# Moving a search's VectorE operands to PSUM and its work into earlier waits, in a balanced expert layer

## The chip, the cores and the metric

The kernel runs on one core of a Trainium2 chip. The metric is the time of one execution on the device in microseconds (us). Runs of one kernel here differ by up to some 1.5%, so all comparisons are between a kernel's fast runs and the runs of the kernel before in the same rounds on the same chip.

## The reference

Linear attention with a root-mean-square norm feeds a layer of eight experts, in which every expert takes exactly 576 of the 4608 tokens. The assignment is greedy over the logits in falling order:

```python
kv = np.einsum('bhsd,bhse->bhde', k, v)                  # batch 8, heads 8, seq 576, dim 64
out = np.einsum('bhsd,bhde->bhse', q, kv)
attn = out / sqrt(mean(out * out) + 1e-06) * g_norm      # -> x: 4608 x 512
...
order = np.argsort(-(x @ w_gate).flatten())              # 4608 * 8 logits
for idx in order:
    tok, e = int(idx) // E, int(idx) % E
    if assigned[tok] >= 0 or counts[e] >= cap:           # cap = 576
        continue
    assigned[tok] = e; counts[e] += 1
for e in range(E):
    out[assigned == e] = np.maximum(x[assigned == e] @ w1[e], 0.0) @ w2[e]
```

## The kernel before: the parts that matter

The kernel doesn't sort. It fills one expert at a time. For each it finds a threshold of the logits by a search of seven steps; in a step TensorE counts, for 32 candidate thresholds at once, how many tokens lie over each, and VectorE picks the interval and compares again. The chosen tokens become a list, GpSimd gathers their rows from DRAM (`xg`), VectorE scales them (`xs`), TensorE transposes them for the expert's matmuls (`xt`; this is the "turn").

All of it for the later experts is woven into TensorE's program between the matmuls of the earlier expert's two layers. A generator yields a distance, in us of TensorE's matmuls, after which its next piece is put into the program; the programs of TensorE, VectorE and ScalarE then have a fixed order.

```python
def threshold(t, over):                      # the search of expert t
    ...
    for s in range(NSTEP):
        yield 4.6 if s > 0 else 0.4 if first else 2.0 if t == 1 else 4.0
        n_ps = bank([P, E, G], "n_ps")
        for c in range(0, GC, G):            # "the counting": nine small matmuls
            nc.tensor.matmul(n_ps, lhsT=over[:, c:c + G]..., rhs=best[:, :, c:c + G], ...)
        ...                                  # VectorE: need, full, some, some_t, kk, ends: the interval
        compare(over, candidates(s + 1, lo, cand_ps))     # "over", 1.35 us, what the next counting reads
...
def fetch(t, which, index):                  # the list
    ...
    yield 3.2 if t == 1 else 4.2 if t < E - 1 else 2.4
    ...                                      # a_ps: matmuls, then know and since on VectorE
    yield 1.6
    ...                                      # s_ps: matmuls, then less, ids, got on VectorE
    for n, (_, nr) in enumerate(blocks):     # five blocks of up to 128 rows
        xg = moe.tile([P, H, W], FT, name="xg", tag="xg", bufs=NB)
        tokens = nc.gpsimd.indirect_dma_start(out=xg[0:nr]..., in_=x_dram, in_offset=...ids...)
    yield "tokens"
    yield 1.5
    ...                                      # up, at_row, half, outs: the rows of the output
def control(t):
    ...                                      # threshold, assign, fetch, later
    for _ in choice():                       # best expert of each token left, for the next search
        yield 0.9
    compare(compared[t + 1], candidates(0, ...))
...
def turn(t):
    def scale(n):
        xs = moe.tile([P, H * D], FT, name="xs", tag="xs")          # two buffers
        nc.vector.tensor_tensor(xs..., xg[0:nr, :, 0:D], xg[0:nr, :, D:D + 1].to_broadcast(...), op=AL.mult)
    scale(0); scale(1)
    yield
    for n, (a, nr) in enumerate(blocks):
        ...                                  # four transposes, ScalarE copies to xt
        if n + 2 < NB:
            scale(n + 2)
        yield
...
hold = 5.0                                   # the turn's first two scalings are put in 5 us after the list
```

## Time and profile before

The kernel took 711.39 us (median of three runs, 709.41 to 716.79). The trace falls into the part up to the first expert's matmuls and eight stretches, one for each expert; stretches 0 to 6 carry the searches and turns. In the lines of profiles below, PE is TensorE (PEld its loading of weights), DVE VectorE, ACT ScalarE and POOL GpSimd. A line of a timeline gives the start and length in us, the engine, the line of the kernel, the operation, output<-inputs, sizes and count, and in brackets the engine's idle time before it and what ended that.

| part of the span before (709.6 us) | us | TensorE busy, us | TensorE idle, us |
|---|---|---|---|
| up to the first matmul of expert 0 | 180.3 | | |
| stretches 0 to 6 | 459.9 | 450.6 | 9.4 |
| rest (stretch 7 and the end) | 69.3 | | |

### The profile page before, as it was taken

Reading aid. Unit: us, or ns where it says so; the run is one execution under the profiler, and the core shown is the slowest. Engines: PE = TensorE matmul, PEld = TensorE weight load, DVE = VectorE, ACT = ScalarE, POOL = GpSimd, SP = SyncE. Lnnn points to the kernel's source line nnn. Section 1 sums busy time; section 2 is a strip of 40 time slices with the busy share of each in tenths; the row PEclk is TensorE's granted clock in tenths of the full one; section 3 lists DMA queues with packets and bytes.
Section 4 is the critical chain, followed back from the end, with each engine's and each line's share of the span. In section 5 each row is a group of like instructions: output and inputs, shape, how many; then the busy total and the mean of one; then the engine's idle time right before and its main releaser. Section 6 shows DMA issues by size and latency. Waiting matters only on the chain.

```text
span 709.6 us, 13280 instructions
## 1 busy us (share of the span) xinstructions
PE 616.8 (87%) x5370; PEld 482.7 (68%) x5370; DVE 443.3 (62%) x1393; ACT 155.9 (22%) x315; POOL 263.8 (37%) x249
## 2 busy tenths in 40 slices
PE   3787788214999899989998999999899999999994
PEld 2566666212778677857885788678677867877782
DVE  4344656888687778888878779887887545020011
ACT  1454555300211121022102111121112022112100
POOL 0100011002342562438344632735263659226322
PEclk9988977555999999999999999999999999999998
DMA  8987889405303600531081053108013843001001
GB/s 283 316 278 237 278 297 351 177 0 184 129 1 103 251 26 1 205 137 38 6 306 67 1 180 132 68 1 312 28 41 127 293 165 106 0 30 38 0 1 67
DMA packets 41405, 93.41 MB, mean 132 GB/s; under 512 B 3456, under 2 KB 3456, under 8 KB 41344
## 3 DMA queue, kind: packets, MB, share of 16 engines
q1 hardware_dynamic: 34752, 72.49, 29.1%
q0 software_dynamic: 5888, 20.06, 8.1%
q8 instruction: 42, 0.69, 0.4%
q14 instruction: 19, 0.16, 0.1%
q10 hardware_dynamic: 704, 0.02, 0.1%
HBM read 72.50 MB, written 20.05 MB: 130 GB/s over the span
## 4 chain that ended last, share of the span: by engine, by line
PE 74%; DVE 13%; issue 6%; DMA 4%; ACT 1%; POOL 1%; POOLq 0%; ACTq 0%; DVEq 0%
PE h_ps L798 35%; PE y_ps L847 20%; PE o_ps L370 3%; PE qt_ps L301 3%; PE y_ps L858 3%; PE kv_ps L313 3%; PE t_ps L747 2%; DVE over L266 2%; DMA xg<-x_dram,ids 2%; PE n_ps L478 2%; DVE xs L733 1%; DMA gw<-in_moe_w_gate_dram 1%; PE warm_ps L625 1%; DVE need L484 1%; DVE held_ps L524 1%
## 5 line engine op out<-in xcount | busy, mean ns | idle before, releaser
L798 PE MATMUL h_ps<-xt,w_sb 128*128 128x288 f32 x1024 | 260.1, 410 | 0.8 <-ACT xt L750 0.8
L798 PEld LDWEIGHTS h_ps<-xt,w_sb 128*128 128x128 f32 x1024 | 190.6, 190 | 55.4 <-issue 5.7
L801 ACT ACTIVATE hid<-h_ps 128x288 f32<-128x288 f32 x128 | 52.6, 411 | 208.1 <-PE h_ps L798 208.1
L847 PE MATMUL y_ps<-tw,sh 128*128 128x256 f32 x384 | 86.5, 380 | 0.0
L847 PEld LDWEIGHTS y_ps<-tw,sh 128*128 128x128 f32 x384 | 72.0, 190 | 9.3
L789 POOL TENSOR_TENSOR sh<-hid 128x512 f32<-128x512 f32 x32 | 41.7, 1303 | 94.4 <-ACT hid L801 94.3
L673 POOL DMA_INDIRECT xg<-x_dram,ids x40 | 38.6, 964 | 82.8 <-DVE ids L668 35.8
L750 ACT ACTIVATE xt<-t_ps,g_col 128x512 f32<-128x512 f32 (+1 forms) x40 | 25.8, 645 | 161.6 <-PE t_ps L747 161.6
L847 PE MATMUL y_ps<-w_sb,hid 128*128 128x256 f32 x256 | 57.8, 381 | 0.0
L266 DVE TENSOR_TENSOR over<-mx,held_ps 128x1152 bf16<-128x1152 f32 x42 | 56.9, 1354 | 1.5
L818 DVE TENSOR_TENSOR y_sb<-y_ps,u 128x512 f32<-128x512 f32 x24 | 16.4, 684 | 63.8 <-PE y_ps L847 63.8
L756 POOL DMA_INDIRECT out_dram<-y_sb,outs x32 | 33.4, 1043 | 52.1 <-issue 36.7
L847 PEld LDWEIGHTS y_ps<-w_sb,hid 128*128 128x128 f32 x256 | 48.1, 190 | 6.6
L524 DVE TENSOR_SCALAR held_ps<-held_ps,width 32x2 f32<-32x2 f32 x144 | 41.3, 287 | 5.3
L779 POOL TENSOR_TENSOR tw<-w_sb 128x512 f32<-128x512 f32 x32 | 39.9, 1269 | 12.4 <-DMA w_sb<-in_moe_w_dram 12.3
L478 PEld LDWEIGHTS <-over 128*128 128x128 bf16 x441 | 17.5, 97 | 38.8 <-DVE over L266 27.5
L370 PE MATMUL o_ps<-kvx,qt 64*64 64x72 f32 x1152 | 32.9, 261 | 9.8 <-issue 9.2
L733 DVE TENSOR_TENSOR xs<-xg 128x512 f32<-128x512 f32 (+1 forms) x40 | 31.9, 809 | 14.7 <-DMA xg<-x_dram,ids 8.1
L478 PE MATMUL n_ps<-best,over 128*128 128x32 bf16 x441 | 19.3, 179 | 21.1 <-DVE over L266 19.2
L370 PEld LDWEIGHTS o_ps<-kvx,qt 64*64 64x64 f32 x1152 | 26.8, 160 | 15.5 <-issue 14.1
L378 DVE TENSOR_REDUCE ms<-sq 128x8 f32<-128x512 f32 x36 | 24.1, 681 | 20.1 <-ACT sq L376 19.9
L327 POOL COPY kvx<-kv 64x512 f32<-64x512 f32 x16 | 9.8, 609 | 71.3 <-DVE kv L321 70.9
(203 smaller groups left out, 831.9 us busy)
## 6 DMA issues: line engine op xcount, KB each, us to landing
w_sb<-in_moe_w_dram SPq DMA_DIRECT2D x16, 1024.0 KB, 6.3
w_sb<-in_moe_w_dram SPq DMA_DIRECT2D x8, 2048.0 KB, 13.3
k_sb<-in_k_dram SPq DMA_DIRECT2D x16, 576.0 KB, 5.4
v_sb<-in_v_dram SPq DMA_DIRECT2D x16, 576.0 KB, 5.8
q_sb<-in_q_dram SPq DMA_DIRECT2D x16, 576.0 KB, 5.6
x_dram<-o_sb SPq DMA_DIRECT2D x16, 576.0 KB, 4.3
x_dram<-o_sb SPq DMA_DIRECT2D x4, 288.0 KB, 4.2
xg<-x_dram,ids POOLq DMA_INDIRECT x40, 5.4
```

What stands on the lines that cost most here:

```text
L266: nc.vector.tensor_tensor(over[:, c0:c1], mx[:, c0:c1].rearrange("p (c o) -> p c o", o=1).to_broadcast([P, c1 - c0, NCAND]), cand[:, 1:NCA ...
L370: nc.tensor.matmul(o_ps[n * HP:(n + 1) * HP, rp, (2 * r2 + l) * W:(2 * r2 + l + 1) * W], lhsT=turned_q[bn][ks, block // 2, l * HP:(l + 1) ...
L478: nc.tensor.matmul(n_ps, lhsT=over[:, c:c + G].rearrange("p c n -> p (c n)"), rhs=best[:, :, c:c + G], start=(c == 0), stop=(c == GC - G))
L524: nc.vector.tensor_scalar(ends[g * QP:(g + 1) * QP], in0=kk, scalar1=width[0:QP, s:s + 1], scalar2=lo_was[0:QP], op0=AL.mult, op1=AL.add)
L673: tokens = nc.gpsimd.indirect_dma_start(out=xg[0:nr].rearrange("p h w -> p (h w)"), out_offset=None, in_=x_dram, in_offset=bass.IndirectOf ...
L733: nc.vector.tensor_tensor(xs[0:nr].rearrange("p (h d) -> p h d", h=H), xg[0:nr, :, 0:D], xg[0:nr, :, D:D + 1].to_broadcast([nr, H, D]), op ...
L756: put = nc.gpsimd.indirect_dma_start(out=out, out_offset=bass.IndirectOffsetOnAxis(ap=ids_of[t][0:nr, n:n + 1], axis=0), in_=y_sb[0:nr, :] ...
L779: in_order(nc.gpsimd.tensor_tensor(o[:, m:m + 2], x[:, m:m + 2], y[:, m:m + 2], op=AL.subtract))
L789: in_order(nc.gpsimd.tensor_tensor(o[:, ms], x[:, ms], y[:, ms], op=op))
L798: nc.tensor.matmul(h_ps, lhsT=w1[:, 2 * (d % 2) + d // 2, f * P:(f + 1) * P], rhs=xt[:, d, cs], start=(d == 0), stop=(d == DC - 1))
L801: nc.scalar.activation(hid[:, f, cs], h_ps, ACT.Relu)
L847: nc.tensor.matmul(p_ps[:, n], lhsT=left[:, f, n * P:(n + 1) * P], rhs=right[:, f], start=(f == 0), stop=(f == FH - 1))
```

## The change

Its intent is twofold. First, GpSimd is busy beside VectorE, and VectorE operations with two operands in SBUF took longer there (`xs` 865 ns in the mean from 181 to 640 us, 690 from 160 to 181 us, where GpSimd did no tensor operation); so each such operation of the search gets an operand in PSUM. Second, the choice for the next search (`choice`) is done inside the waits for the list, in place of behind it, and the computation of the output's rows is cut into six pieces (`deferred`) that go one by one into the next search's steps. The distances are shortened to match.

```diff
-    def bank(shape, nm):
-        return psm.tile(shape, FT, name=nm, tag="c", bufs=1)
+    given = psm.tile([P, 512], FT, name="given_ps", tag="c", bufs=1)
     held = psm.tile([P, 512], FT, name="held_ps", tag="s", bufs=1)
...
+    for nm, shape in (("n", (E, G)), ("all", (3, E)), ("a", (GC + 1,)), ("rise", (2, GC)), ("inv", (2, H)), ("s", ...)):
+        small_ps[nm] = given[:, at:at + n]
...
-            yield 4.6 if s > 0 else 0.4 if first else 2.0 if t == 1 else 4.0
-            n_ps = bank([P, E, G], "n_ps")
+            yield 4.6 if s > 0 else 0.4 if t < 2 else 2.4
+            n_ps = small_ps["n"]
...
+                if deferred:
+                    deferred.pop(0)()
...
-        yield 5.4
+        yield 5.0 if t == 1 else 5.4
...
-    def fetch(t, which, index):
+    def fetch(t, which, index, later):
+        ch = choice() if 0 < t < E - 1 else iter(())
...
-        yield 3.2 if t == 1 else 4.2 if t < E - 1 else 2.4
+        if t > 0:
+            later()
+        yield 2.8 if t < E - 1 else 2.4
...
-        yield 1.6
+        next(ch, None)
+        yield 1.3
...
-            yield 1.5
+            yield 0.7
...
+        deferred.extend([lambda: ...code_left, lambda: climb(0), lambda: climb(1), ...at, half_rows, rows])
+        for _ in ch:
+            yield 0.5
...
+            inv = xg[:, :, D:D + 1]
+            if t > 0:
+                inv = small_ps["inv"][:, n % 2].rearrange("p (h o) -> p h o", o=1)
+                nc.vector.tensor_copy(inv[0:nr], xg[0:nr, :, D:D + 1])
             nc.vector.tensor_tensor(xs[0:nr]..., xg[0:nr, :, 0:D],
-                                    xg[0:nr, :, D:D + 1].to_broadcast([nr, H, D]), op=AL.mult)
+                                    inv[0:nr].to_broadcast([nr, H, D]), op=AL.mult)
```

`held` is a bank that only VectorE uses.

More of the change, by code (lines that the diff above doesn't have):

```diff
@@ L449 @@
                       ("own", (GC,)), ("shut", (E,)), ("code", (E,)), ("some", (2 * QP,)), ("some_t", (2, QP + 1)),
-                      ("kk", (2,)), ("which", (1,)), ("over_room", (E,)), ("last", (E,)), ("is_full", (E,))):
+                      ("kk", (2,)), ("which", (1,)), ("over_room", (E,)), ("last", (E,)), ("is_full", (E,)), ("half", (NB,))):
         n = shape[0] * (shape[1] if len(shape) > 1 else 1)
@@ L455 @@
         at += n
+    at = 0
+    for nm, shape in (("n", (E, G)), ("all", (3, E)), ("a", (GC + 1,)), ("rise", (2, GC)), ("inv", (2, H)), ("s", (NB, GC + 3))):
+        n = shape[0] * (shape[1] if len(shape) > 1 else 1)
+        small_ps[nm] = given[:, at:at + n]
+        if nm == "s":
+            small_ps["mid"] = given[:, at:at + E * GC].rearrange("p (e c) -> p e c", e=E)
+        if len(shape) > 1:
+            small_ps[nm] = small_ps[nm].rearrange("p (t n) -> p t n", t=shape[0])
+        at += n
+    nc.vector.tensor_copy(small_ps["rise"], rise)
     nc.vector.memset(small_ps["some_t"][0:QP, 0, QP:QP + 1], 1.0)
@@ L464, in pieces @@
         return sm[:, 0:2], sm[:, 2:]
+    deferred = []
     def threshold(t, over):
@@ L545, in assign @@
             nc.vector.scalar_tensor_tensor(cut[:, 1], in0=mx, scalar=ends[1], in1=cut[:, 1], op0=AL.is_ge, op1=AL.mult)
-        two = asg.tile([P, 2, E, GC], BF, name="two", tag="two")
-        for n in range(2):
-            nc.vector.tensor_tensor(two[:, n], best, bc_c(cut[:, n]), op=AL.mult)
+        upper, mid = asg.tile([P, E, GC], BF, name="upper", tag="upper"), small_ps["mid"]
         sums = small("sums", 2 * E, BF)
-        with nc.allow_low_precision("counts of up to GC are exact in bf16"):
-            nc.vector.reduce_sum(out=sums, in_=two.rearrange("p t e c -> p (t e) c"), axis=AXX)
-        yield 5.4
-        all_ps = bank([P, 3, E], "all_ps")
+        for n, part in enumerate((upper, mid)):
+            nc.vector.tensor_tensor(part, best, bc_c(cut[:, n]), op=AL.mult)
+            with nc.allow_low_precision("counts of up to GC are exact in bf16"):
+                nc.vector.reduce_sum(out=sums[:, n * E:(n + 1) * E], in_=part, axis=AXX)
+        for do in deferred:
+            do()
+        deferred.clear()
+        yield 5.0 if t == 1 else 5.4
+        all_ps = small_ps["all"]
         nc.tensor.matmul(all_ps[:, 0], lhsT=ones_b, rhs=sums[:, 0:E], start=True, stop=True)
@@ L558, in assign @@
         nc.tensor.matmul(all_ps[:, 2], lhsT=before, rhs=sums[:, E:2 * E], start=True, stop=True)
-        mid = two[:, 1]
         here = asg.tile([P, E, GC], FT, name="here", tag="here")
@@ L589, in later @@
                 nc.vector.tensor_copy(small_ps["code"], code)
-            nc.vector.scalar_tensor_tensor(gone, in0=took, scalar=NONE, in1=gone, op0=AL.mult, op1=AL.add)
+            nc.vector.tensor_scalar(small_ps["mine"], in0=took, scalar1=NONE, scalar2=None, op0=AL.mult)
+            nc.vector.tensor_tensor(gone, gone, small_ps["mine"], op=AL.add)
             nc.vector.tensor_scalar(room, in0=over_room, scalar1=0.0, scalar2=None, op0=AL.max)
@@ L640, in fetch @@
         nc.vector.tensor_tensor_scan(along, ones_b[:, 0:GC], own, 0.0, op0=AL.mult, op1=AL.add)
-        yield 3.2 if t == 1 else 4.2 if t < E - 1 else 2.4
-        a_ps = bank([P, GC + 1], "a_ps")
+        if t > 0:
+            later()
+        yield 2.8 if t < E - 1 else 2.4
+        a_ps = small_ps["a"]
         nc.tensor.matmul(a_ps[:, 0:1], lhsT=before, rhs=along[:, GC - 1:GC], start=True, stop=True)
@@ L652, in fetch @@
             nc.vector.tensor_tensor(since, slot_f, a_ps[:, 0:1].to_broadcast([P, NB * P]), op=AL.is_ge)
-        yield 1.6
-        s_ps = bank([P, NB, GC + 3], "s_ps")
+        next(ch, None)
+        yield 1.3
+        s_ps = small_ps["s"]
         for n in range(NB):
@@ L683, in fetch, with climb, half_rows, rows @@
             yield "tokens"
-            yield 1.5
+            yield 0.7
         up = asg.tile([P, NB, 2, GC], FT, name="up", tag="up")
-        for n in range(2):
-            nc.vector.tensor_tensor(up[:, :, n], less, rise[:, n].rearrange("p (o c) -> p o c", o=1).to_broadcast([P, NB, GC]),
-                                    op=AL.mult)
         at = asg.tile([P, NB, 2], FT, name="at_row", tag="at_row")
-        nc.vector.reduce_sum(out=at, in_=up, axis=AXX)
-        half = small("half", NB)
-        nc.vector.tensor_scalar(half, in0=at[:, :, 1], scalar1=S - 1.0, scalar2=-(S - 1.0), op0=AL.mult, op1=AL.add)
-        nc.vector.tensor_tensor(half, half, got[:, :, 1], op=AL.mult)
-        nc.vector.tensor_tensor(half, half, at[:, :, 0], op=AL.add)
+        half = small_ps["half"]
         outs = asg.tile([P, NB], I32, name="outs", tag="outs", bufs=3)
-        nc.vector.scalar_tensor_tensor(outs, in0=got[:, :, 0], scalar=float(R), in1=half, op0=AL.mult, op1=AL.add)
         ids_of[t] = outs
-        nc.vector.scalar_tensor_tensor(code_left, in0=code, scalar=which, in1=code_left, op0=AL.not_equal, op1=AL.mult)
+        def climb(n):
+            nc.vector.tensor_tensor(up[:, :, n], less, (rise if t == 0 else small_ps["rise"])[:, n].rearrange(
+                "p (o c) -> p o c", o=1).to_broadcast([P, NB, GC]), op=AL.mult)
+        def half_rows():
+            nc.vector.tensor_scalar(half, in0=at[:, :, 1], scalar1=S - 1.0, scalar2=-(S - 1.0), op0=AL.mult, op1=AL.add)
+            nc.vector.tensor_tensor(half, half, got[:, :, 1], op=AL.mult)
+        def rows():
+            nc.vector.tensor_tensor(half, half, at[:, :, 0], op=AL.add)
+            nc.vector.scalar_tensor_tensor(outs, in0=got[:, :, 0], scalar=float(R), in1=half, op0=AL.mult, op1=AL.add)
+        deferred.extend([
+            lambda: nc.vector.scalar_tensor_tensor(code_left, in0=code if t == 0 else small_ps["code"], scalar=which,
+                                                   in1=code_left, op0=AL.not_equal, op1=AL.mult),
+            lambda: climb(0), lambda: climb(1), lambda: nc.vector.reduce_sum(out=at, in_=up, axis=AXX), half_rows, rows])
+        if t == 0:
+            later()
+        if not 0 < t < E - 2:
+            for do in deferred:
+                do()
+            deferred.clear()
+        for _ in ch:
+            yield 0.5
     compared = {0: over0}
@@ L710, in control @@
             yield "weights"
-        yield from fetch(t, which, index)
-        later()
-        pause = None if t == 0 else 0.9
-        if t + 1 < E:
+        yield from fetch(t, which, index, later)
+        if t == 0:
             for _ in choice():
-                yield pause
-            yield pause
+                yield None
+        yield None if t == 0 else 0.5
         if t + 1 < E - 1:
```

## The prediction

> **What bounds the kernel now**
>
> I read the page first (engine shares and the chain that ended last), then the busy time by stretch, with one stretch for each expert's two matmul layers, then the timeline of TensorE for its pauses, and last the timelines of VectorE, GpSimd and the DMA around those pauses. Stretch k below is the layers of the k-th expert (0 to 7), in which the search for a later expert is woven into TensorE's program.
>
> ```profile
> PE 616.8 (87%) x5370; PEld 482.7 (68%) x5370; DVE 443.3 (62%) x1393; ACT 155.9 (22%) x315; POOL 263.8 (37%) x249
> ...
> PE 74%; DVE 13%; issue 6%; DMA 4%; ACT 1%; POOL 1%; POOLq 0%; ACTq 0%; DVEq 0%
> ```
>
> TensorE carries 74% of the chain. The stretches (columns: window, length, then busy time and count of PE, PEld, DVE, ACT, POOL, granted clock, DMA share, GB/s):
>
> ```profile
> 180.30:250.40 70.10, 67.74 (x368) 52.17 (x368) 52.05 (x173) 12.12 (x25) 30.30 (x26) 0.98 0.35 124
> 250.40:317.00 66.60, 64.25 (x353) 50.10 (x351) 55.22 (x176) 11.55 (x24) 29.66 (x25) 1.00 0.27 94
> 317.00:383.30 66.30, 64.47 (x362) 50.36 (x360) 52.82 (x177) 11.55 (x24) 32.91 (x29) 1.00 0.29 104
> ...
> 578.70:640.30 61.60, 61.60 (x284) 48.49 (x284) 18.86 (x30) 11.56 (x24) 31.61 (x27) 1.00 0.23 75
> ```
>
> TensorE is busy for nearly the whole of every stretch at a granted clock of 0.98 to 1.00. Stretch 6, without a search step, takes 61.6 us; those with one take 63 to 70. All that better scheduling can win there is TensorE's pauses, and from 240 us on the timeline of TensorE shows six (the bracket is the pause and what ended it):
>
> ```profile
> 239.31 0.66 PE L747 MATMUL t_ps<-ident,xs 128*128 128x128 f32 x4 [2.32 <-DVE xs L733]
> 305.85 0.66 PE L747 MATMUL t_ps<-ident,xs 128*128 128x128 f32 x4 [2.35 <-DVE xs L733]
> 377.39 0.63 PE L747 MATMUL t_ps<-ident,xs 128*128 128x128 f32 x4 [1.83 <-DVE xs L733]
> 440.42 0.63 PE L747 MATMUL t_ps<-ident,xs 128*128 128x128 f32 x4 [0.36 <-DVE xs L733]
> 454.13 0.39 PE L478 MATMUL n_ps<-best,over 128*128 128x32 bf16 x9 [0.21 <-DVE over L266]
> 496.46 0.39 PE L478 MATMUL n_ps<-best,over 128*128 128x32 bf16 x9 [0.42 <-DVE over L266]
> ```
>
> These six add up to 7.49 us, 1.1% of the span. Nearly all of it is the turn of the next expert's tokens waiting for VectorE's scaling (xs). At the first turn matmuls at half pace cost about 1.3 us more (4 matmuls took 1.69 us at 239.97 in the chain of waits, where 4 take 0.87). So **the ceiling of the gain is about 8.8 us, 1.2%**; faster by over 2% is out of reach.
>
> [...]
>
> [...] The first group is of 160 to 181 us, where GpSimd did no tensor operation; the second is of 181 to 640 us:
>
> ```profile
> L733 DVE TENSOR_TENSOR xs<-xg 128x512 f32<-128x512 f32 x4 | 2.8, 690 | 1.2 <-DMA xg<-x_dram,ids 1.0 <-PE t_ps L747 0.2
> L561 DVE TENSOR_TENSOR_SCAN here<-inner,two 128x288 f32<-128x288 bf16 x1 | 0.7, 747 | 0.0
> ...
> L733 DVE TENSOR_TENSOR xs<-xg 128x512 f32<-128x512 f32 x28 | 23.7, 865 | 13.3 <-DMA xg<-x_dram,ids 7.1 <-PE t_ps L747 6.2
> L561 DVE TENSOR_TENSOR_SCAN here<-inner,two 128x288 f32<-128x288 bf16 x6 | 5.0, 832 | 0.0
> ```
>
> [...] the bf16 product "two" took 301 ns with SBUF operands in search 0 and 449 with one in PSUM later. [...] My main argument rests on this: a wait at the head of VectorE's queue holds everything behind it.
>
> **The change part by part**
>
> *PSUM operands.* The scaling factors, the slopes and "mid" move to PSUM. By the means above xs loses 0.18 us (865-690) x 28 = 4.9 us, "up" 0.53 us (868-335) x 14 = 7.5 us, the scan and the operation after it 0.09 x 6 and 0.15 x 6 = 1.4 us. That is 14 us of VectorE, which is 62% busy; it lies beside TensorE except before a turn. Added: a copy of 8 columns ahead of each of 35 scalings (about 0.15 us, as the 10-column copy got) and, in each search, one more reduction of about 0.45 us. In search 0, where nothing hides it, the fp32 product (+0.15), the split sum (+0.15) and the scan, which now waits for the counting (+0.3), cost 0.6 us.
>
> *Shorter waits in the program.* The programmed distances around the list shrink: counting to list from 9.1 us to 6.9 us in the second layer, and the next search starts 13 matmul pairs after the list, where it started about 27. A pair is 0.495 us in the first layer (20 records in 4.95 us), 0.434 in the second, and the nine counts of a step take 0.22.
>
> *What the list then costs.* Take the counting matmuls of a search as T. From the scan to "along" search 0 needed 4.48 us (162.27 to 166.75), all of it now after the counting: T+4.7, against nine pairs (4.46): a pause of 0.2. Six short updates (0.9) now stand before "know", then know and since (1.0): T+6.6, against three more pairs (1.49): a pause of 0.35. Then wl and its maximum (1.1) and the list's own operations (1.1): ids at T+8.85. That is 0.5 us of pauses in each of stretches 1 to 4: 2.0 us.
>
> *What the moved choice costs.* Its rest takes 2.1 us, comparison and candidates 1.6: T+12.6, in time for the first counting of the next search at T+13.2. But the build's order puts both scalings, xs 0 and 1, directly behind, ahead of the first "need". They wait for the gathered rows, and the FIFO holds the search. GpSimd issues gather 0 at T+9.1 and gather 1 at T+10.4. Before, the third list went so:
>
> ```profile
> 423.61 0.99 POOL L673 DMA_INDIRECT xg<-x_dram,ids  x1 [1.70 <-DVE got L670]
> ...
> 430.53 0.68 DVE L733 TENSOR_TENSOR xs<-xg 128x512 f32<-128x512 f32 x1
> 431.64 0.69 DVE L733 TENSOR_TENSOR xs<-xg 128x512 f32<-128x512 f32 x1 [0.43 <-DMA xg<-x_dram,ids]
> ...
> 434.51 0.15 DVE L484 TENSOR_TENSOR need<-goal,n_ps 32x8 f32<-32x8 f32 x1
> ...
> 437.65 1.35 DVE L266 TENSOR_TENSOR over<-mx,held_ps 128x1152 bf16<-128x1152 f32 x1
> ```
>
> Issue to landing of gather 1 was 6.7 us (424.90 to 431.61); the median in the five stretches is 4.6 to 6.9. So xs 1 ends at T+10.4+6.7+0.85 = T+18.0, need to the end of over is 4.45, and the second step is ready at T+22.4. TensorE stands at it at T+13.2+0.2+4.95 = T+18.4. **The pause is 4.0 us at a landing of 6.7, 1.9 at 4.6.** Before, that step came later and TensorE never noticed.
>
> By stretch: in 0 the second step stands behind the turn's second transpose, list+13.4, ready at list+16.5: 3.1 us (0.8 at the short landing), and the scaling for the third transpose comes behind that step (2.25 us of VectorE, 0.3 of TensorE): 1.95. In 1 the gathers also wait for GpSimd's second block of sums (about 2.4 us): 4.0, and about 1.0 at the third transpose. In 2: 4.0, and 2.3 at the third transpose, as the fourth step stands directly before the turn. In 3: 4.0. In 4 the list comes 6 us into the stretch, and in GpSimd's order the gathers stand behind the differences tw, which in the stretch that began at 448.0 ended at 462.5: gather 1 is issued at 15.9 and lands near 19.3 (3.4 us, about the shortest landing, since the weights have come), the step is ready at 24.6 and wanted at 18.4: 6.2.
>
> Sum: 2.0 + (3.1+4.0+4.0+4.0+6.2) + (1.95+1.0+2.3) = 28.5 us of new pauses; with short landings (0.8, 2.0, 1.9, 1.9, 6.2) about 20. Minus 8.8 removed, plus 0.6 in search 0: **+12 to +20 us**, that is 723 to 732.
>
> **The rivals**
>
> *The intended one:* the turn's pauses go and nothing replaces them, 711.4 - 7.5 + 0.6 = 704 to 706. For it: the distances look fitted to VectorE's undisturbed durations, and all steps but the second have slack (5.17 us for about 4.7). Against it: it needs the gathers to land within about 3 us of issue, and the fourth stretch's gathers to pass tw. *Hidden anyway:* the landings are early and only some of the pauses arise, so gain and loss cancel: 708 to 718. *GpSimd's gain carries on:* its operations are slightly shorter without contention and puts leave earlier; but no pause of TensorE ends on GpSimd, so this is worth nothing by itself.
>
> **Range and chances**
>
> The mechanism alone gives about 728 with an error of some 6 us. I give it 0.7, and 0.3 to the other two at about 708, since distances so finely set were probably tried out. The prediction is 724 us, the range 705 to 734. Slower by over 2% means over 725.6: about 0.68 of the mechanism's share, 0.47 in all. Faster by over 2%, 0.02.
>
> **What would show it right or wrong**
>
> Right: TensorE's pauses before the first transpose of a turn are gone; pauses of 2 to 6 us stand before the second counting step of the next search in stretches 0 to 4, ended by over, with VectorE idle for "DMA xg" just before; the one in stretch 4 is the longest and GpSimd's tw lies before its gathers; xs falls from 865 to about 690 ns. Wrong: if no pause of TensorE is ended by over, or the gathers land within 3 us, the time falls near 705. If the pauses are there but the xs that ends them is not waiting for the DMA, the sizes are right by accident.

The premises about the chip, as the runs show them:

- A wait at the head of VectorE's queue: in e1 (experiment 1) the first counting of stretch 0 had ended at 232.21 us, and the `need` that reads it began at 237.27, behind two scalings, the first of which had waited 2.88 us for its rows.
- Operands in PSUM: that `xs` and `up` would lose all of their extra time beside GpSimd was an estimate, which the trace of the kernel before doesn't show. In the changed kernel they took 687 and 334 ns in the mean, for 865 and 868. The added reduction, an estimate of 0.45 us, took 453 ns.
- Landings: in the kernel before, gathers landed 3.3 to 7.0 us after their issue (median 5.4). The two issued at 423.61 and 424.90 us, with a DMA share of 1.04 until 430.4, took 6.8 and 6.7; the one issued at 591.24, with a share of 0.45, took 3.6.
- GpSimd's own operations: the largest group of `sh` took 1303 ns in the mean before and 1268 in the changed kernel.

## More of the kernel before

The number to watch is the idle time of TensorE in stretches 0 to 6: the sum of the pauses that the change wants to remove. It is the length of the stretches less TensorE's busy time.

## The result, and the profile after

The changed kernel took 752.79 us (median of four runs, 748.49 to 755.8); the kernel before, with one more run beside them, 710.4. The ratio is 1.058, with a 95% interval of 1.0487 to 1.0674: slower.

The page of the changed kernel, engines and chain of waits:

```profile
PE 622.9 (83%) x5370; PEld 483.8 (65%) x5370; DVE 438.9 (59%) x1443; ACT 155.5 (21%) x315; POOL 258.4 (35%) x249
...
PE 63%; DVE 19%; issue 6%; DMA 6%; POOL 3%; ACT 2%; POOLq 0%; DVEq 0%; ACTq 0%
```

VectorE has less work than before (438.9 us against 443.3), yet its share of the chain rose from 13% to 19%, that of the DMA from 4% to 6%, and TensorE's fell from 74% to 63%. TensorE waits more. How much, and in which form, the busy times of stretches 0 to 6 show. First their sum in the kernel before:

```profile
sum 459.92, PE 450.56 PEld 350.75 DVE 328.89 ACT 81.47 POOL 218.94; mean PE 64.37 PEld 50.11 DVE 46.98 ACT 11.64 POOL 31.28
```

Then three of the stretches of the changed kernel, and the sum of the same seven (the columns are those of the stretches in the prediction; the clock is the third number from the end):

```profile
176.55:252.22 75.67, 68.26 (x377) 52.17 (x377) 59.84 (x198) 12.10 (x25) 29.02 (x26) 0.98 0.31 108
...
327.80:405.31 77.51, 69.43 (x371) 53.02 (x369) 60.30 (x207) 11.54 (x24) 32.55 (x29) 0.93 0.26 94
...
554.13:615.77 61.64, 61.64 (x285) 48.53 (x283) 17.63 (x52) 11.54 (x24) 31.07 (x28) 1.00 0.36 122
sum 500.87, PE 462.91 PEld 357.34 DVE 324.68 ACT 81.32 POOL 213.58; mean PE 66.13 PEld 51.05 DVE 46.38 ACT 11.62 POOL 30.51
```

The seven stretches grew by 40.9 us (500.87 - 459.92), about the whole difference of the medians. (The two profiled runs differ by 37.1 us, since the part before the stretches was 3.8 us shorter in the changed kernel's; that part varies by 8.8 us between the profiled runs.) Of this, 28.6 us is idle time of TensorE: 37.96 after, 9.36 before. The other 12.3 us is TensorE being busy for longer (462.91 against 450.56) with the same number of matmuls, at a clock of 0.93 to 0.98 in stretches 0 to 4. Stretch 5, at a clock of 1.00, takes no longer than its matmuls.

Where the idle time lies, the timeline of TensorE shows. Five pauses make 25.95 of the 37.96 us:

```profile
234.93 0.38 PE L490 MATMUL given_ps<-best,over 128*128 128x32 bf16 x9 [4.70 <-DVE xs L772]
...
299.36 0.40 PE L490 MATMUL given_ps<-best,over 128*128 128x32 bf16 x9 [5.65 <-DVE xs L772]
...
363.50 0.40 PE L490 MATMUL given_ps<-best,over 128*128 128x32 bf16 x9 [4.67 <-DVE xs L772]
...
432.10 0.40 PE L490 MATMUL given_ps<-best,over 128*128 128x32 bf16 x9 [4.68 <-DVE xs L772]
...
500.42 0.40 PE L490 MATMUL given_ps<-best,over 128*128 128x32 bf16 x9 [6.25 <-DVE xs L772]
500.66 7.22 PE L837 MATMUL h_ps<-xt,w_sb 128*128 128x288 f32 x20
...
507.95 5.10 PE L837 MATMUL h_ps<-xt,w_sb 128*128 128x288 f32 x20
```

Each stands before the first counting of the next search, and each is ended by a scaling, `xs`. That is odd at first sight: the counting reads `best` and `over`, and VectorE had finished `over` long ago. VectorE at the first of the pauses:

```profile
228.40 1.35 DVE L266 TENSOR_TENSOR over<-mx,held_ps 128x1152 bf16<-128x1152 f32 x1
232.65 0.18 DVE L771 COPY given_ps<-xg 128x8 f32<-128x8 f32 x1 [2.90 <-DMA xg<-x_dram,ids]
...
234.18 0.69 DVE L772 TENSOR_TENSOR xs<-xg,given_ps 128x512 f32<-128x512 f32 x1
```

`over` is ready at 229.8. VectorE then stands for 2.90 us with the first scaling's copy at the head of its queue, waiting for the gathered rows, and the second scaling ends at 234.9: there the counting begins. The link between the two that the program shows is the PSUM bank: the scaling reads `inv` in the bank `given`, and the counting writes `n` into it. That TensorE's write waits there for VectorE's earlier accesses to the bank was my guess, which this trace alone doesn't show. The first experiment tests it.

The busy part shows in the last two lines of TensorE's timeline. The 20 matmuls right behind the pause of 6.25 us took 7.22 us; the next 20 of the same kind took 5.10. The windows of 500 to 503 us and of 506 to 512 us give the clock that was granted:

```profile
500.00:503.00 3.00, 2.58 (x14) 2.00 (x14) 2.23 (x11) 0.00 (x0) 0.00 (x0) 0.50 0.34 124
...
506.00:512.00 6.00, 6.00 (x34) 4.68 (x33) 3.44 (x14) 1.23 (x3) 4.97 (x4) 1.00 0.00 0
```

It was 0.50 behind the pause and 1.00 a little later. In the trace's record of the clock, half clock lasted from 498.15 us, 3.98 us into the pause, to 504.97, after 4.55 us of work from the end of the pause at 500.42. Each of the five pauses is followed by about 2 us of such loss (half of TensorE's busy time at half clock: 1.7 to 2.5 us, 10.9 in all), and the pause of 3.20 us before a transpose of stretch 2 by 1.6. That is 12.4 us, where the kernel before lost 1.7 in one place: 10.7 of the 12.3 us; the rest I didn't trace. **These six pauses were charged twice: 29.15 us for their length, and 12.4 for half a clock after them.**

What the change was to win, it did win on VectorE. The groups of stretches 0 to 6:

```profile
L772 DVE TENSOR_TENSOR xs<-xg,given_ps 128x512 f32<-128x512 f32 x26 | 17.9, 687 | 4.1 <-PE t_ps L786 2.7
L714 DVE TENSOR_TENSOR up<-less,given_ps 128x180 f32<-128x180 f32 x14 | 4.5, 334 | 0.0
L771 DVE COPY given_ps<-xg 128x8 f32<-128x8 f32 x26 | 4.5, 173 | 34.7 <-DMA xg<-x_dram,ids 34.4
```

`xs` fell from 865 to 687 ns and `up` from 868 to 334 (a mean that one operation sets, see experiment 2), but 34.4 us of VectorE's waiting now stands ahead of the small copies, for the gathers.

### The profile page after: what moved, and what is told of

Same layout as the page of the kernel before. It is cut to its first block, busy times and chain, and to the rows that moved or that the text cites. A ratio compares the mean times of both kernels' runs of the same rounds, so it can differ in the third digit from the quotient of the medians.

```text
span 746.7 us, 13342 instructions
## 1 busy us (share of the span) xinstructions
PE 622.9 (83%) x5370; PEld 483.8 (65%) x5370; DVE 438.9 (59%) x1443; ACT 155.5 (21%) x315; POOL 258.4 (35%) x249
## 4 chain that ended last, share of the span: by engine, by line
PE 63%; DVE 19%; issue 6%; DMA 6%; POOL 3%; ACT 2%; POOLq 0%; DVEq 0%; ACTq 0%
PE h_ps L837 28%; PE y_ps L886 19%; DMA xg<-x_dram,ids 5%; PE y_ps L897 3%; PE qt_ps L301 3%; PE o_ps L370 3%; PE kv_ps L313 3%; DVE over L266 2%; PE given_ps L490 2%; PE t_ps L786 2%; DVE xs L772 1%; DVE held_ps L536 1%; POOL tw L818 1%; DMA gw<-in_moe_w_gate_dram 1%; DVE need L496 1%
## 5 line engine op out<-in xcount | busy, mean ns | idle before, releaser
L837 PE MATMUL h_ps<-xt,w_sb 128*128 128x288 f32 x1024 | 266.6, 417 | 0.8 <-ACT xt L789 0.8
L837 PEld LDWEIGHTS h_ps<-xt,w_sb 128*128 128x128 f32 x1024 | 194.8, 194 | 56.9 <-issue 4.9
L886 PE MATMUL y_ps<-tw,sh 128*128 128x256 f32 x384 | 88.8, 386 | 0.0
L828 POOL TENSOR_TENSOR sh<-hid 128x512 f32<-128x512 f32 x32 | 40.6, 1268 | 103.0 <-ACT hid L840 102.9
L490 PE MATMUL given_ps<-best,over 128*128 128x32 bf16 x441 | 19.4, 180 | 48.4 <-DVE xs L772 27.1
L795 POOL DMA_INDIRECT out_dram<-y_sb,outs x32 | 31.3, 977 | 62.5 <-issue 37.4
L864 POOL TENSOR_TENSOR y_sb<-u,u 128x512 f32<-128x512 f32 x8 | 10.1, 1267 | 104.8 <-DVE u L857 62.7
L818 POOL TENSOR_TENSOR tw<-w_sb 128x512 f32<-128x512 f32 x32 | 39.9, 1266 | 12.3 <-DMA w_sb<-in_moe_w_dram 12.1
L370 PE MATMUL o_ps<-kvx,qt 64*64 64x72 f32 x1152 | 31.4, 251 | 6.4 <-issue 5.4
L313 PE MATMUL kv_ps<-v_sb,k_sb 64*64 64x64 f32 x1152 | 28.3, 241 | 9.5 <-issue 9.5
```

Source lines behind the costliest of these rows:

```text
L313: nc.tensor.matmul(kv_ps[cs, l, r * D:(r + 1) * D], lhsT=k_sb[ls, r, j, :], rhs=v_sb[ls, r, j, :], start=(j < 2), stop=(j >= R - 2))
L370: nc.tensor.matmul(o_ps[n * HP:(n + 1) * HP, rp, (2 * r2 + l) * W:(2 * r2 + l + 1) * W], lhsT=turned_q[bn][ks, block // 2, l * HP:(l + 1) ...
L490: nc.tensor.matmul(n_ps, lhsT=over[:, c:c + G].rearrange("p c n -> p (c n)"), rhs=best[:, :, c:c + G], start=(c == 0), stop=(c == GC - G))
L795: put = nc.gpsimd.indirect_dma_start(out=out, out_offset=bass.IndirectOffsetOnAxis(ap=ids_of[t][0:nr, n:n + 1], axis=0), in_=y_sb[0:nr, :] ...
L818: in_order(nc.gpsimd.tensor_tensor(o[:, m:m + 2], x[:, m:m + 2], y[:, m:m + 2], op=AL.subtract))
L828: in_order(nc.gpsimd.tensor_tensor(o[:, ms], x[:, ms], y[:, ms], op=op))
```

## The experiments

All are built from the changed kernel unless said otherwise, and all but one give the right result. Theory A: the loss is that VectorE's queue stands behind the wait for the gathered rows, while TensorE waits for something later in that queue; the shared bank only sets at which counting, and the clock adds its part. The kernel before had medians of 712.14, 712.9 and 710.44 us in the three sets.

| run | median us | ratio to before | idle of TensorE, stretches 0-6 | busy there |
|---|---|---|---|---|
| changed kernel | 752.79 | 1.058 | 37.96 | 462.91 |
| e1_inv_held | 748.37 | 1.0514 | 34.06 | 463.46 |
| e2_sched_only | 759.55 | 1.0681 | 46.32 | 463.45 |
| e3_psum_only | 717.22 | 1.0085 | 14.46 | 453.24 |
| e4_warm_pause | 747.50 | 1.0506 | 20.36 | 476.84, of it 20.25 unneeded |
| e5_spaced6 | 721.80 | 1.0129 | 15.01 | 453.48 |
| e6_spaced5 | 732.56 | 1.027 | 18.96 | 461.14 |
| e7_late_scale | 726.75 | 1.0205 | 19.98 | 454.44 |
| e8_no_gather_wait | 723.71 | 1.0144 | 19.05 | 453.94 |
| e9_spaced6_xs3 | 713.13 | 1.0047 | 8.92 | 451.83 |
| e10_spaced76_xs3 | 708.45 | 0.9967 | 5.44 | 450.50 |
| e11_before_xs3 | 710.42 | 0.9995 | 8.80 | 450.50 |
| e12_psum_xs3 | 714.08 | 1.0042 | 11.49 | 452.61 |

(Idle is the sum of the seven stretches less TensorE's busy time in them, from the profiled run; before it is 9.36 and 450.56.)

### 1. `inv` out of TensorE's bank

```diff
-    held: ... ("half", (NB,))
-    given: ("n", (E, G)), ("all", (3, E)), ("a", (GC + 1,)), ("rise", (2, GC)), ("inv", (2, H)), ("s", ...)
+    held: ... ("half", (NB,)), ("inv", (2, H))
+    given: ("n", (E, G)), ("all", (3, E)), ("a", (GC + 1,)), ("rise", (2, GC)), ("s", ...)
```

> The changed kernel with one edit: the scaling factors (inv) lie in the PSUM bank that TensorE never writes, in place of the bank of the counts. In the changed kernel TensorE stood 4.70, 5.65, 4.67, 4.68 and 6.25 us before the FIRST counting of the next search, ended by xs. Theory A (shared bank on top of VectorE's queue): TensorE's count waits there only because it writes the bank that the scalings read; with inv moved the first counting does not wait, but the search still stands behind the gathers in VectorE's queue, so 3 to 5.5 us each appear before the SECOND counting, ended by over: about 20 us in place of 26, time 743 to 750. Rival B (the shared bank is the whole cost): no pause takes their place, time 708 to 722. Rival C (TensorE waits there for something else that VectorE does): pauses stay before the first counting, time 750 to 756.

Measured: 748.37 us, 1.0514 (1.0456 to 1.0573). No first counting waits any more. Instead the second one does, in the same five stretches, for 2.83, 4.42, 3.76, 4.25 and 7.58 us, ended by `over`. Stretch 0 as an example:

```profile
241.82 0.41 PE L490 MATMUL given_ps<-best,over 128*128 128x32 bf16 x9 [2.83 <-DVE over L266]
244.18 1.08 PE L786 MATMUL t_ps<-ident,xs 128*128 128x128 f32 x4 [1.96 <-DVE xs L772]
```

So `inv` in TensorE's bank was what moved the pause to the first counting. It cost about 4 us of pauses (37.96 against 34.06, one trace each; the intervals of the two ratios overlap). As `given` is one tile and one bank, this doesn't tell whether the build keeps the order by the tile or by the bank. The pause is there without it: the first step's operations on VectorE still stand behind the two scalings. The two pauses shown are nearly the figures of the prediction, 3.1 and 1.95 in this stretch.

### 2. The order alone

The order and the distances of the change, but `rise`, `inv` and `mid` in SBUF as before (`half`, `code` and the product for `gone` stay in PSUM):

```diff
-        upper, mid = asg.tile([P, E, GC], BF, name="upper", tag="upper"), small_ps["mid"]
+        two = asg.tile([P, 2, E, GC], BF, name="two", tag="two")
+        mid = two[:, 1]
...
-            nc.vector.tensor_tensor(up[:, :, n], less, (rise if t == 0 else small_ps["rise"])[:, n]...
+            nc.vector.tensor_tensor(up[:, :, n], less, rise[:, n]...
...
-            if t > 0:
-                inv = small_ps["inv"][:, n % 2].rearrange("p (h o) -> p h o", o=1)
-                nc.vector.tensor_copy(inv[0:nr], xg[0:nr, :, D:D + 1])
```

> The changed kernel's order of instructions with the operands of before: slopes, scaling factors and mid in SBUF, one product and one reduction of both halves. Theory A: the order alone makes nearly all of the loss; pauses of 3 to 6 us before the second counting in five stretches, xs near 0.8 us by contention; 740 to 750. Rival B (sharing the bank is the whole cost): 704 to 714, below or at before.

Measured: 759.55 us, 1.0681 (1.0643 to 1.0719), slower than expected. It is above the changed kernel's ratio too, but the two intervals overlap. The pauses before the second counting are there (2.57 to 8.58 us, 23.9 in all), so the order makes a loss of this size by itself. Longer VectorE operations beside GpSimd come on top, by more than I had expected. One `up`, and the GpSimd operations under it:

```profile
262.61 6.78 DVE L712 TENSOR_TENSOR up<-less,rise 128x180 f32<-128x180 f32 x1
```

```profile
264.25 2.50 POOL L813 TENSOR_TENSOR tw<-w_sb 128x512 f32<-128x512 f32 x2
266.70 2.48 POOL L813 TENSOR_TENSOR tw<-tw,w_sb 128x512 f32<-128x512 f32 x2
```

An operation whose shortest time in this run was 0.34 us took 6.78, over the GpSimd operation that was running and the five behind it of some 1.25 us each, and ended just as GpSimd's block of eight subtractions did (269.39 and 269.18 us). It held the next counting for 5.97 us. Three more operations with two SBUF operands, a scan of 5.66 us and an `up` of 5.74 and one of 6.49, also lasted until such a block ended (the scan 0.6 us longer). In the order before, `up` stood in another place, and took 0.33 to 0.41 us in eleven of fourteen cases. But the kernel before has one such case too, in stretch 6, where no counting follows:

```profile
585.14 6.15 DVE L688 TENSOR_TENSOR up<-less,rise 128x180 f32<-128x180 f32 x1
```

It sets most of the mean of 868 ns from which the prediction took `up`'s gain, and it cost TensorE nothing. So the two halves of the change belong together: with the rows' operations moved, `up` took up to 6.78 us with both operands in SBUF, and 0.331 to 0.335 us in all fourteen cases with one in PSUM (the changed kernel; the one at 258.09 us ran under such a block). Against the run before (order the same, operands in PSUM), the time is 1.5% longer (759.55 us against 748.37, in the same rounds; the intervals don't overlap).

### 3. The operands alone

The kernel before, its order and distances, with the PSUM operands of the change in the shared bank.

```diff
-            n_ps = bank([P, E, G], "n_ps")
+            n_ps = small_ps["n"]
...
+                inv = small_ps["inv"][:, n % 2].rearrange("p (h o) -> p h o", o=1)
+                nc.vector.tensor_copy(inv[0:nr], xg[0:nr, :, D:D + 1])
```

> The kernel before with its own order and waits, but with the PSUM operands of the change, in the same shared bank. Theory A: there the scalings already stood ahead of the first counting, which came late enough, so sharing the bank costs little: no pause above 3 us, xs at 0.69 us, time 705 to 715. Rival B: 730 or more.

Measured: 717.22 us, 1.0085 (1.0054 to 1.0116): a little over the range. Three countings wait for a scaling (0.75, 1.48 and 0.35 us, 2.6 together), which the kernel before never shows. One of them:

```profile
449.95 0.38 PE L488 MATMUL given_ps<-best,over 128*128 128x32 bf16 x9 [1.48 <-DVE xs L747]
```

So the shared bank makes TensorE wait here too, for 2.6 of the 5.1 us by which the idle time grew (14.46 against 9.36). VectorE's shorter operations gain nothing that TensorE waited for.

### 4. Work in the pause

To test the clock: 18 unneeded matmuls right before the first counting of searches 2 to 6, in which TensorE would otherwise be idle.

```diff
+            if s == 0 and t > 1:
+                warm(18, "t", 1)
```

> The changed kernel with 18 unneeded bf16 matmuls of 512 columns (about 0.21 us each at full pace, 3.9 us) put before the first counting of searches 2 to 6, where TensorE stood still. If matmuls after a pause run at half pace because of the pause (20 first-layer records took 7.22 us after the last one, 4.95 elsewhere; about 11 us over the five), this takes about 8 to 11 us off though it adds work: 741 to 746, with those 20 records at about 4.95 us. If the slow matmuls have another cause: 750 to 756.

Measured: 747.50 us, 1.0506 (1.0455 to 1.0557), between the two ranges; the interval overlaps that of the changed kernel, so the time alone shows no gain. The trace does show one of pace: TensorE was at half clock for 13.7 us of the stretches, where it was for 34.1 in the changed kernel. In the table, idle time and unneeded work are together 40.61 us, 2.65 more than the idle time of the changed kernel; the needed work (476.84 - 20.25 = 456.59) is 6.3 us less. So half of the 12.3 us was indeed recovered, while the added matmuls gave 2.65 back. It is not more because the 4.05 us of work (18 matmuls of 0.225 us) didn't fill every pause:

```profile
497.02 4.05 PE L644 MATMUL warm_ps<-wide,ones_b 128*128 128x512 bf16 x18
503.48 0.38 PE L492 MATMUL given_ps<-best,over 128*128 128x32 bf16 x9 [2.41 <-DVE given_ps L773]
503.71 6.79 PE L839 MATMUL h_ps<-xt,w_sb 128*128 128x288 f32 x20
```

Behind the 2.41 us that were left, 20 matmuls again took 6.79 us. Where a pause was only 0.79 us, 20 of the same kind behind it took 5.10 us.

### 5 and 6. The first counting later

If Theory A holds, the search needs only to start after the gathered rows have landed. With `inv` in `held` in both:

```diff
-            yield 4.6 if s > 0 else 0.4 if t < 2 else 2.4
+            yield 4.6 if s > 0 else 0.4 if t < 2 else 6.4     # e6: 5.0
```

> The changed kernel with inv in the bank of VectorE's own tiles, and the first counting of a search from the third on 4.0 us of TensorE work later (a distance of 6.4 in place of 2.4), so that the comparison behind it comes to VectorE after the gathered rows have landed. Theory A (the loss is that VectorE stands in its queue behind the wait for the gathered rows while TensorE waits for a count): the five pauses of 2.8 to 7.6 us before the second counting, 22.8 us in all, fall under 5 us together, the half pace behind them goes as well, the last search still ends before its list is asked for, and the time is 705 to 718 us. Rival B (the search has no slack left; a later start moves the same pauses to the choice or to the wait for the weights): pauses appear at its end and the time stays at 738 us or more.

Measured: 721.80 us, 1.0129 (1.0058 to 1.02). The pauses before the second counting are gone (one counting of another step waits for 0.28 us), and with them most of the half clock: the busy time is back at 453.48 us, and the loss by half clock is 3.4 us in place of 12.4. Rival B is out. The time is 4 us over the range. Pauses of 13.7 us are left before the transposes of the turn (the expectation of e9 says 12.7). In stretch 0, for one, the third scaling came before the first step's operations on VectorE, and the fourth behind them.

```profile
240.28 0.63 PE L786 MATMUL t_ps<-ident,xs 128*128 128x128 f32 x4 [0.81 <-DVE xs L772]
...
246.01 0.63 PE L786 MATMUL t_ps<-ident,xs 128*128 128x128 f32 x4 [4.23 <-DVE xs L772]
```

> As the run before with a distance of 5.0 in place of 6.4. Theory A: the pauses before the second counting shrink by about the 2.6 us by which the counting moves, four of the five (2.8, 4.4, 3.8, 4.3 us) to under 2 us and the 7.6 one to about 5; time 715 to 728 us. Rival B: 738 us or more.

Measured: 732.56 us, 1.027 (1.0179 to 1.0361), over its range, and between e1 and e5 as the distance is. The second counting waits 0.23 and 0.40 us in stretches 1 and 2 and 2.89 in stretch 4; in stretch 0 it doesn't wait, but a transpose does, for 5.15 us. The clock was 0.93 and 0.94 in stretches 0 and 4, so that busy time was 461.14 us. The clock's own record says how: TensorE is at half clock in blocks of 3.41 us, here seven (10.9 us lost; two of them behind the pause of 5.15 us and two behind one of 2.74), in e5 two (3.4 us lost). Over stretches 0 to 6 of the fourteen traces such a block begins in or within 3.5 us behind all 17 pauses of 3.6 us and more, 21 of the 35 of 2.0 to 3.4 us, and 3 of the 96 shorter ones. What decides between 2.0 and 3.4 us isn't shown: of two pauses of the kernel before, the stretch with 2.32 us had a clock of 0.98, that with 2.35 us 1.00.

### 7. The scalings later

The other way to keep the wait for the gathers out of the search's way: the scalings given out behind the first step.

```diff
-            hold, turning = 5.0, None
+            hold, turning = 5.0 if t == 0 else 10.0, None     # and inv in held
```

> The changed kernel with inv in the bank of VectorE's own tiles, and the two scalings of the gathered rows given out 10 us of TensorE work after the list in place of 5, so that the first step's operations stand ahead of them in VectorE's queue. Theory A: the pauses before the second counting fall from 22.8 us to under 8 us; the transposes that need the scaled rows may wait a little longer (up to 2 us a layer); time 715 to 730 us. Rival B (it is the number of VectorE's operations between two countings, whatever it waits for): pauses of 3 us and more stay, time 740 us or more.

Measured: 726.75 us, 1.0205 (1.0132 to 1.0278), in the range of Theory A. In stretches 1 to 4 the pauses before the second counting are gone (20.0 us in e1), and the third counting waits there for 4.4 us, ended by an `up`. Stretch 0, which the edit leaves out, kept its pause of 2.82 us (2.83 in e1). The two scalings and copies that moved are 1.7 us of VectorE's work, and each of the four stretches lost 2.9 to 5.3 us of pauses, so Rival B's reading, by which only the number of operations counts, fails. The transposes wait for 11.1 us in all, as the scalings now come late for them.

### 8. No wait for the gathers

The changed kernel as it is, the bank shared, with a wrong result: the scaling reads a resident tile of ones, so that no scaling waits for a gather.

```diff
+    stand_in = asg.tile([P, H, W], FT, name="stand_in", tag="stand_in")
+    nc.vector.memset(stand_in, 1.0)
...
+            if t > 0:
+                xg = stand_in
```

> The changed kernel as it is, with a result that is wrong on purpose: from the second layer on the scaling reads a resident tile of ones in place of the gathered rows, so that VectorE never waits for a gather, while the gathers still run. Theory A: the five pauses before the first counting (4.7 to 6.3 us, 26 us in all) fall under 3 us together, the half pace behind them goes too, and the time is 705 to 720 us. Rival C (what holds the first counting is the bank it shares with the scaling, or VectorE's own work ahead of it, and not the transfer): pauses of 3 us or more stay and the time is 735 us or more.

Measured: 723.71 us, 1.0144 (1.0059 to 1.0229). The five pauses before the first counting fell from 26 to 5.3 us (1.31, 0.88, 1.02, 1.02, 1.03), and busy time from 462.91 to 453.94. What is left of them is the two scalings themselves, behind which the bank makes TensorE wait. That is more than the 3 us that I had put down, and the time is 4 us over the range, but nearer to Theory A than to Rival C on both counts: the wait for the transfer made 21 of the 26 us.

### 9 and 10. A third buffer for the scaled rows

e5 left the transposes. In these two the third scaling is given out with the first two, and the later ones one block earlier.

```diff
-            xs = moe.tile([P, H * D], FT, name="xs", tag="xs")
+            xs = moe.tile([P, H * D], FT, name="xs", tag="xs", bufs=3)
...
         scale(1)
+        if t > 0:
+            scale(2)
...
-            if n + 2 < NB:
-                scale(n + 2)
+            if len(scaled) < NB:
+                scale(len(scaled))
# and the first distance 6.4 (e9) or 7.6 (e10), inv in held
```

> The later first counting (distance 6.4, inv in VectorE's own bank) and a third buffer for the scaled rows, so that the third scaling stands ahead of the first step in VectorE's queue and the fourth too, in place of behind it. Theory A: of the 14.7 us of pauses of the run with 6.4, the 12.7 before the turn's transposes, which wait for a scaling that stands behind the first step's operations, fall under 4 us; 8 to 12 us with the slower matmuls behind them; time 706 to 714 us, at the time before or a little under. Rival D (the transposes wait for the gathers themselves): the pauses stay and the time is 718 us or more.

Measured: 713.13 us, 1.0047 (1.0004 to 1.009), in the range. The pauses before transposes fell from 13.7 to 3.8 us; one of 3.22 us in stretch 0 is most of it.

> As the run before with a distance of 7.6 in place of 6.4: if the first step still collides with the scalings the time falls by 2 to 5 us more; if it doesn't, it stays within 2 us of it, and if the search's end gets late, pauses before the choice or the list show and it rises.

Measured: 708.45 us, 0.9967 (0.9918 to 1.0016), the lowest, 4.7 us less than e9 (the two intervals just overlap). The sum of its stretches 0 to 6:

```profile
sum 455.94, PE 450.50 PEld 349.15 DVE 325.25 ACT 81.47 POOL 213.68; mean PE 64.36 PEld 49.88 DVE 46.46 ACT 11.64 POOL 30.53
```

5.44 us of idle time are left of 37.96, and TensorE's busy time is that of before, with no half clock in these stretches. So the loss of the changed kernel is accounted for: later countings, a bank of VectorE's own and one buffer take it back whole. As a gain on the kernel before it isn't shown: the interval holds 1.

### 11 and 12. The same buffer without the order

> The kernel before with nothing but the third buffer for the scaled rows. Its pauses before the turn's transposes are 8.7 us in five places. If they wait for the buffer or VectorE's queue, 4 to 7 us of them go: 704 to 709 us. If they wait for the gathers or the list: 711 to 714.

The kernel before with the third buffer alone: 710.42 us, 0.9995 (0.9954 to 1.0036). The time is between the two ranges; three transposes still wait for 2.32, 1.56 and 2.35 us. No gain of the buffer alone is shown.

> The order and waits of the kernel before with all PSUM operands of the change, inv in VectorE's own bank (so that the counting no longer waits for a scaling) and the third buffer. The run with the PSUM operands alone was at 717; its pauses before the countings ended by a scaling were 2.6 us and those before transposes 10.2. Expected: 706 to 712; if the operands cost something apart from the shared bank, 715 or more.

The operands of the change with the order before, `inv` in `held` and the third buffer: 714.08 us, 1.0042 (0.9994 to 1.0089). This is over the range, and under the 715 that was to mean a cost of the operands themselves; it is undecided. No counting waits for a scaling any more, which was the bank's doing in e3, but four wait for `over` (5.1 us). Why they do, when e11 shows 2.2, I leave open.

## Why the prediction was right or wrong

**Right: the bound and the ceiling.** TensorE's pauses and its pace make the difference in every run of the table; the best version, e10, gained some 4 us in the stretches where the ceiling was said to be 8.8. The ceiling was read a little low: a seventh pause was missed,

```profile
509.51 0.63 PE L747 MATMUL t_ps<-ident,xs 128*128 128x128 f32 x4 [1.86 <-DVE xs L733]
```

and the half pace at the first turn cost 1.7 us by the clock's record, so that it is 9.4 + 1.7 = 11.1 us.

**Right: the VectorE durations.** `xs` came to 687 ns for a predicted 690, `up` to 334 for 335, the scan to 752 and the copy to 173 for about 150. As said, this lay beside TensorE and was worth little: with the order before (e3) it won nothing. Most of `up`'s expected gain of 7.5 us is the one operation of 6.15 us in stretch 6.

**Right: the pauses before a turn's first transpose went**, and GpSimd's `tw` delays the gathers in stretch 4, where it ran until 493.6 us and gather 0 was issued at 493.79. That stretch has the longest pause, 6.25 us.

**Right: the cause of the loss.** The strict order of VectorE's queue, the scalings at its head and the search behind them were the main argument, and e5, e7 and e8 each took the wait away in another way and got most of the time back (721.80, 726.75 and 723.71 us, for 752.79).

**Wrong: "in time for the first counting of the next search at T+13.2".** The comparison was in time (at the first pause `over` was ready at 229.8 us), but the counting began only at 234.93, behind the scalings that read its bank. By the prediction's own figures, the second scaling ends at T+18.0, so the pause should have stood at the first counting and been 4.8 us, in place of 4.0 at the second. Five such pauses came to 25.95 us for a predicted 21.3. e1 gave the bank back, and the pauses went where the prediction had put them, with 22.84 us in sum.

**Wrong: the sum, which charged the pauses at their length alone.** The prediction saw half pace in the kernel before (1.3 us at the first turn) and counted it only as something to win, never behind its own five new pauses. This is the largest miss: 12.3 us more of busy time, where the sum expected 1.3 less. e4 recovered 6.3 of it by keeping TensorE at work.

**Wrong in size: the smaller terms.** The list's counting was to cost 2.0 us of pauses and cost 0.59 in one place. The third and later transposes were to cost 5.25 us and cost 8.62. Other countings had 2.03 us of pauses that were not foreseen. With the first countings, this makes 37.2 us of new pauses where the prediction had 28.5.

Together: idle time grew by 28.6 us where the sum has 21.0 (28.5 less 7.5), and busy time by 12.3 where it has 1.3 less. These 7.6 and 13.6 us are what lies between the 40.9 us by which the stretches grew and the 19.7 us that the sum has for them (28.5 - 8.8). **Wrong as well: the weight of 0.3 for the rivals.** "Distances so finely set were probably tried out" pulled the figure down; the mechanism alone had said 728. (Weighed by 0.7 and 0.3, 728 and 708 give 722, not 724.)

## What to carry to other kernels

Before work is moved into an earlier slot of a strict queue, ask what stands at the head of that queue then: here two short operations that waited for a transfer held a search for 4 to 6 us. All 17 pauses of TensorE of 3.6 us and more were charged here with some 1.4 to 2.9 us on top for the slower matmuls behind them, and 21 of the 35 of 2.0 to 3.4 us had half clock behind them too: an estimate should allow for it. A bank that TensorE writes was a poor place for VectorE's own operands here: writes to one part of it began only behind reads of another, 4.67 to 6.25 us late in five places, and no first counting waited once `inv` lay in another bank (e1). And look at the single operations behind a mean before a gain is worked out from it.
